# Three output tiles for the last chunk and a first load from a second queue, in a fused recurrence and feed-forward kernel

## The chip, the cores and the metric

The kernel runs on one core of one Trainium2 chip. The core has five engines, each with its own stream of instructions: TensorE (PE; PEld is its weight load), VectorE (DVE), ScalarE (ACT), GpSimd (POOL) and SyncE (SP, which here only issues transfers). They work beside each other and wait for one another through semaphores. Sixteen DMA engines move data between the chip's main memory and the core's memory, SBUF; a transfer is started by an instruction on an engine's queue (SPq and ACTq in the profile). Matmuls write to PSUM, which DVE and ACT can read.

The metric is the device time in microseconds (us) of one execution. The kernel before took 250.95 us, the median of three timed runs (249.91 to 251.05).

## The reference

```
def _attn_ref(r, k, v, w, a, b):          # each (4, 8, 768, 40), float32
    for t in range(S):
        y[:, :, t] = einsum('bhd,bhde->bhe', rt, state)
        Sa = einsum('bhde,bhe->bhd', state, at)
        state = state * wt[:, :, None, :] - einsum('bhd,bhe->bhde', Sa, bt) \
                + einsum('bhd,bhe->bhde', vt, kt)

def _moe_ref(x, w_in, w_out):             # x: y turned to (3072, 320)
    h = x @ w_in                          # 320 -> 2048
    r = maximum(h, 0)
    return (r * r) @ w_out                # 2048 -> 320, float32
```

A recurrence over 768 steps for 32 heads, with a decay `w` in each step, gives `y`; its rows go through a feed-forward layer of two matrix products with a squared ReLU between them. The output is 3072 rows of 320.

## The kernel before

The 768 steps are cut into 12 chunks of 64 (`L`, `NCH`), numbered `c` from 0 to 11. For each chunk, `load(c)` brings in six inputs, `prep(c)` takes the logarithm of the decay (`ln`, line 530), splits it into two bf16 parts (`hi`, line 369, and `lo`, line 384), sums it over time with triangular matmuls and applies exponentials; `rec(c)` solves the chunk and moves the state on; `read(c)` forms `y`, and `ffn(c)` puts it through the layer. Before chunk 0 nothing can begin without the decay: `ln 0` waits for both halves of `raw_w`, 64 partitions each, which `load` issues one after the other from SP (line 411). ScalarE's own first instruction is the load of its function table (line 270); VectorE's first are memsets of padding (lines 313 and 318), and `hi 0` stands behind them.

In `ffn(c)`, `F`/`FL` are the products with `w_in` (256 tokens in the columns), `f` the ReLU from PSUM into the buffer `G` and `q` its square, each in four parts `u0` to `u3` of four blocks of 128 hidden units. `O c` is the product with `w_out`: for each of the 16 hidden blocks and each half `g` of the tokens one matmul of 128 tokens by 320 output columns, summed over the blocks in PSUM, so 32 matmuls a chunk in four parts. `o c` copies the result to SBUF (`osb`), and `st c` stores it.

PSUM is used as four slots of two banks each (`slot`, tiles `pb0` to `pb3`). A result that takes a slot is given its number by the order; in the tile of `O c` the half `g0` lies in one bank and `g1` in the other.

Nothing is scheduled at run time: `Plan.add` records each operation with what it reads and writes, and `plan.issue(ORDER)` emits them in the order of the long string `ORDER` (lines 87 to 215). An entry such as `PE2 O 11 u0` means: on PE, into slot 2, operation `O 11 u0`; `SP st 10` means that SP issues the store of chunk 10. Each engine runs its entries in that order; semaphores are added between engines wherever the tiles demand it, and a PSUM tile counts as one thing: a reader of one half waits for all writes issued to the tile before it, and readers on two engines follow one another.

The last chunk, 11, has its own end (lines 932 to 962). The fourth part of its output product is issued by halves, `OL 11 g1` and then `OL 11 g0`; each half is then evicted in two pieces of 160 columns, `o0` by ACT (line 374) and `o1` by DVE (line 369), and stored by two transfers of 63 rows, `st0` from SP and `st1` from ACT (line 960). Its end in the order is

```
PE2 O 11 u0; DVE o 10; PE O 11 u1; SP st 10; PE O 11 u2; PE OL 11 g1; PE OL 11 g0;
ACT o0 11 g1; DVE o1 11 g1; ACT o0 11 g0; DVE o1 11 g0;
ACT st1 11 g0; ACT st1 11 g1; SP st0 11 g1; SP st0 11 g0
```

Of the kernel before, what the change touches and what calls it, by code (L numbers as in the profile page):

```python
# [209 lines left out]
ACT f 10 u2; DVE f 10 u1; PE1 F 11 u2; ACT q 10 u2; DVE q 10 u1; PE0 FL 11 u1; PE2 FL 11 u3; DVE q  # L210
10 u0; PE FL 11 u2; PE FL 11 u0; PE F 11 u3; ACT f 11 u0; PE F 11 u1; ACT f 11 u2; PE3 O 10 u0;
ACT q 11 u2; PE O 10 u1; ACT f 11 u1; PE O 10 u2; ACT f 11 u3; POOL q 11 u1; ACT q 11 u0; PE O 10
u3; ACT q 11 u3; PE2 O 11 u0; DVE o 10; PE O 11 u1; SP st 10; PE O 11 u2; PE OL 11 g1; PE OL 11
g0; ACT o0 11 g1; DVE o1 11 g1; ACT o0 11 g0; DVE o1 11 g0; ACT st1 11 g0; ACT st1 11 g1; SP st0
11 g1; SP st0 11 g0"""


@with_exitstack
def kernel(
# [30 lines left out]
    def rows(g):  # L250
        return slice(64 * g, 64 * g + 64)
# [150 lines left out]
    def load(c):  # L402
        t0 = slice(c * L, c * L + L)

        def half(x, g):
            return x[2 * g:2 * g + 2, :, t0, :].rearrange("b h t e -> t (b h) e")

        for nm, x, ring in (("w", w, raw_w),):
            def go(x=x, ring=ring):
                for g in range(2):  # L410
                    nc.sync.dma_start(out=ring[c % len(ring)][rows(g)], in_=half(x, g))
            plan.add(f"ld{nm} {c}", [("SP", 2400)], ("ew", {"SP": go}),
                     writes=[("raw", nm, c % len(ring))])

        for y, (nm, x) in enumerate((("k", k), ("b", b))):
            def go_runs(y=y, x=x):
                xv = x[:, :, t0, :].rearrange("b (p q) (k i) e -> q (b p) k (i e)", q=2, i=8)
                for q in range(2):
                    nc.sync.dma_start(out=runs_of(c, y)[:, q, :], in_=xv[q])
            if c in RUNS:  # L420
                plan.add(f"ld{nm} {c}", [("SP", 1100)], ("ew", {"SP": go_runs}),
                         writes=[("raw", nm, c % NKBR)])
                continue
# [13 lines left out]

        def go_a():
            xv = a[:, :, t0, :].rearrange("b (p q) (k i) e -> q (b p) k (i e)", q=2, i=8)
            for q in range(2):  # L440
                nc.sync.dma_start(out=raw_a[c % NA][:, q, :], in_=xv[q])
        plan.add(f"lda {c}", [("SP", 1100)], ("ew", {"SP": go_a}), writes=[("raw", "a", c % NA)])


        def go_r():
            to = raw_r[c % NR]
            if c < NCH - 1:
                xv = r[:, :, c * L + 1:c * L + L + 1, :].rearrange(
                    "b (p q) (k i) e -> q (b p) k (i e)", q=2, i=8)
                for q in range(2):  # L450
                    nc.sync.dma_start(out=to[:, q, :], in_=xv[q])
                return

            x0, pair, m = (c * L + 1) * D, 2 * T * D, NH // 2 - 1
            for q in range(2):
                s0 = x0 + q * T * D
                xv = r.rearrange("b h t e -> (b h t e)")[s0:s0 + m * pair].rearrange(
                    "(m x) -> m x", x=pair)[:, 0:L * D].rearrange("m (k f) -> m k f", f=8 * D)
                nc.sync.dma_start(out=to[0:8 * m, q, :], in_=xv)
                xl = r[NB - 1, NHH - 2 + q, c * L + 1:T, :].rearrange("t e -> (t e)")  # L460
                nc.sync.dma_start(out=to[8 * m:8 * m + 7, q, :],
                                  in_=xl[0:56 * D].rearrange("(k f) -> k f", f=8 * D))
                nc.sync.dma_start(out=to[8 * m + 7:8 * m + 8, q, 0:7 * D],
                                  in_=xl[56 * D:63 * D].rearrange("(k f) -> k f", k=1))
        plan.add(f"ldr {c}", [("SP", 1100 if c < NCH - 1 else 3000)], ("ew", {"SP": go_r}),
                 writes=[("raw", "r", c % NR)])
# [406 lines left out]
    def ffn(c):  # L873
        q2 = c % 2
        for u in range(NFB // 4):
# [24 lines left out]
            for x in (1, 0) if tail else (0, 1):  # L900
# [18 lines left out]
                    out=gv, in_=gv, func=ACTF.Square))],  # L919
               reads=[("G", q2, u)], writes=[("G", q2, u)])  # L920
        ho = ("O", c)
        for u in range(NFB // 4):
            ms = [[], []]
            for j in range(4 * u, 4 * u + 4):
                for g in range(2):
                    ms[g].append(mm(
                        lambda g=g: slot(ho, FP32)[:, g, 0:DM],
                        lambda g=g, j=j: G[q2][:, j, 2 * g * L:2 * g * L + 2 * L],
                        lambda j=j: WOUT[:, j, :], j == 0, j == NFB - 1))
            rd = ([("G", q2, x) for x in range(max(u, O_AFTER) + 1)]  # L930
                  + [("WOUT", 2 * u), ("WOUT", 2 * u + 1)])
            if c == NCH - 1 and u == NFB // 4 - 1:

                for g in range(2):
                    pe(f"OL {c} g{g}", "D", DM, ms[g], reads=rd, writes=[ho + (g,)])
            else:
                pe(f"O {c} u{u}", "D", DM, [m for x in zip(*ms) for m in x], reads=rd,
                   writes=[ho, ho + (0,), ho + (1,)], alloc=[ho] if u == 0 else [])
        ov = out.rearrange("(g bb s) f -> bb s g f", g=2, bb=2)
        t0, n = c * L + 1, min(L, T - 1 - c * L)  # L940
        if c < NCH - 1:
            ew(f"o {c}", copy_alts(lambda: osb[q2][:], lambda: slot(ho, FP32)[:, :, 0:DM], 2 * DM),
               reads=[ho, ho + (0,), ho + (1,)], writes=[("osb", q2)], free=[ho])

            def store():
                for bb in range(2):
# [1 line left out]
            plan.add(f"st {c}", [("SP", 1500)], ("ew", {"SP": store}), reads=[("osb", q2)],  # L948
                     writes=[("left", c)])
            return  # L950
        h = DM // 2
        for g in range(2):
            for x, e in enumerate(("ACT", "DVE")):
                ew(f"o{x} {c} g{g}", copy_alts(
                    lambda g=g, x=x: osb[q2][:, g, h * x:h * x + h],
                    lambda g=g, x=x: slot(ho, FP32)[:, g, h * x:h * x + h], h, engines=(e,)),
                   reads=[ho + (g,), ("left", c - 2)], writes=[("osb", q2, g, x)], free=[ho])
            for bb, (e, q) in enumerate((("SP", nc.sync), ("ACT", nc.scalar))):
                plan.add(f"st{bb} {c} g{g}", [(e, 750 if e == "SP" else 60)],
                         ("ew", {e: lambda q=q, bb=bb, g=g: q.dma_start(  # L960
                             out=ov[bb, t0:t0 + n, g], in_=osb[q2][64 * bb:64 * bb + n, g])}),
                         reads=[("osb", q2, g, 0), ("osb", q2, g, 1)])

    def weights():

# [97 lines left out]
```

## Time and profile before

| | us |
|---|---|
| median of three timed runs | 250.95 (249.91 to 251.05) |
| the profiled execution | 249.74 |
| its span, first to last instruction | 248.0 |
| PE busy | 223.8 (90%) |
| DVE busy | 189.1 (76%) |
| ACT busy | 178.0 (72%) |
| POOL busy | 110.1 (44%) |
| mean granted TensorE clock | 0.987 |

All views below come from the one profiled execution. The page cuts the span into 40 equal slices and shows in each the busy share in tenths; `PEclk` is the clock that TensorE was granted, `DMA` the mean busy share of the 16 DMA engines. The chain is the work that ended last, followed back step by step to what released it. The timeline lists instructions by start, with their length, line and tiles; in brackets stands the idle time of the engine before them and what ended it. Names such as `pb<-WOUT,G` give the tile written and those read; `128x320` is partitions by elements. A row that ends in x64 merges 64 instructions. Where a wait has several semaphores, the profile names the one that came last.

### The profile page before, as it was taken

What the parts mean: (1) busy time and instruction counts of PE and PEld (TensorE: products, weight loads), DVE (VectorE), ACT (ScalarE), POOL (GpSimd) and SP (SyncE); (2) the same over time, 40 slices, a digit from 0 to 9 for tenths busy, and PEclk for the clock granted to TensorE, in tenths of its full rate; (3) what the DMA queues carried; (4) which work ended last, traced back from release to release, by engine and by line L of the source; (5) the groups of instructions that cost most, each with busy time, mean ns of one, the idle gap of its engine ahead of it and who ended that gap; (6) DMA issues with size and microseconds to landing.
All of it is one profiled execution on the core that took longest, in us unless ns stands there. A gap on an engine that the chain in (4) does not pass through costs nothing.

```text
span 248.0 us, 12188 instructions
## 1 busy us (share of the span) xinstructions
PE 223.8 (90%) x5568; PEld 177.3 (71%) x5568; DVE 189.1 (76%) x236; ACT 178.0 (72%) x236; POOL 110.1 (44%) x110
## 2 busy tenths in 40 slices
PE   0588677599999999999999999999999999999991
PEld 0377666488787877788878877877788787867770
DVE  7698988359987889898869696999897578854411
ACT  2588889569899687868777887774777773944850
POOL 4144024532765716473870991491279900033030
PEclk9999999979999999999999999999999999999997
DMA  5989899989999969769698099995410000302021
GB/s 131 209 216 206 168 200 259 328 145 214 181 215 207 152 150 168 138 128 181 136 183 166 14 219 152 193 176 119 119 47 3 3 5 15 96 5 56 0 50 55
DMA packets 102152, 33.54 MB, mean 135 GB/s; under 512 B 88918, under 2 KB 101718, under 8 KB 101846
## 3 DMA queue, kind: packets, MB, share of 16 engines
q1 hardware_dynamic: 101958, 32.62, 63.0%
q8 instruction: 43, 0.70, 1.3%
q10 hardware_dynamic: 144, 0.16, 0.2%
q14 instruction: 7, 0.06, 0.1%
HBM read 28.84 MB, written 3.93 MB: 132 GB/s over the span
## 4 chain that ended last, share of the span: by engine, by line
PE 74%; DVE 9%; DMA 6%; ACT 4%; issue 3%; POOL 1%; SPq 1%; ACTq 0%
PE pb L388 63%; PE pb L392 7%; PE pb L395 4%; DMA G<-in_moe_w_in_dram 3%; DVE KBT L510 2%; DMA raw_a<-in_a_dram 2%; DVE AR L643 1%; DMA out_dram<-osb 1%; POOL WIN L378 1%; ACT G L908 1%; DVE STb L318 1%; DVE VU L371 1%; DVE lo L384 1%; DVE EN L669 1%; ACT osb L374 1%
## 5 line engine op out<-in xcount | busy, mean ns | idle before, releaser
L388 PE MATMUL pb<-WOUT,G 128*128 128x320 bf16 x384 | 57.1, 299 | 0.0
L916 POOL TENSOR_TENSOR G<-G 128x1024 bf16<-128x1024 bf16 x19 | 36.2, 1913 | 39.7 <-PE pb L392 19.3
L388 PE MATMUL pb<-XT,WIN 128*128 128x256 bf16 x384 | 49.9, 279 | 0.0
L908 ACT ACTIVATE G<-pb 128x1024 bf16<-128x1024 f32 x37 | 37.4, 1022 | 14.3 <-PE pb L388 13.1
L388 PEld LDWEIGHTS <-G 128*128 128x128 bf16 x384 | 35.9, 98 | 13.8 <-issue 0.5
L388 PEld LDWEIGHTS <-WIN 128*128 128x128 bf16 x384 | 35.6, 99 | 8.0 <-issue 2.6
L669 DVE TENSOR_TENSOR CX<-pb,MSKI 128x1024 bf16<-128x1024 f32 x24 | 28.9, 1220 | 12.1 <-PE pb L388 11.9
L382 POOL TENSOR_TENSOR KB<-raw_kb,iG 128x640 bf16<-128x640 f32 x14 | 21.6, 1542 | 24.3 <-ACT iG L553 19.9
L669 DVE TENSOR_TENSOR EN<-pb,MSK 128x1024 bf16<-128x1024 f32 x24 | 29.1, 1217 | 3.2 <-PE pb L388 3.1
L559 ACT ACTIVATE Gin<-pb 64x320 f32<-64x320 f32 x48 | 20.2, 428 | 9.4 <-PE pb L388 8.9
L378 POOL CAST VU<-raw_v 64x640 bf16<-64x640 f32 x20 | 14.3, 713 | 16.0 <-DMA raw_v<-in_v_dram 15.6
L761 DVE TENSOR_TENSOR STb<-pb,GT 64x640 bf16<-64x640 f32 x22 | 18.1, 820 | 1.4 <-PE pb L388 0.8
L388 PEld LDWEIGHTS <-EN 64*64 64x64 bf16 x768 | 14.5, 110 | 5.8 <-issue 4.8
L918 ACT ACTIVATE G<-G 128x1024 bf16<-128x1024 bf16 x17 | 17.7, 1055 | 0.1
L643 DVE TENSOR_TENSOR AR<-pb,GT 128x512 bf16<-128x512 bf16 x24 | 15.6, 683 | 2.7 <-PE pb L395 1.7
L374 ACT ACTIVATE osb<-pb 128x640 f32<-128x640 f32 (+1 forms) x10 | 6.2, 623 | 15.2 <-PE pb L388 14.7
L910 DVE TENSOR_SCALAR G<-pb 128x1024 bf16<-128x1024 f32 x11 | 13.4, 1222 | 4.7 <-PE pb L388 4.1
L388 PE MATMUL pb<-XT,WLAST 64*128 64x256 bf16 x192 | 16.8, 271 | 0.0
L382 POOL TENSOR_TENSOR lo<-lnW,hi 128x640 bf16<-128x640 f32 x6 | 8.9, 1492 | 15.8 <-ACT hi L374 10.3
L388 PE MATMUL pb<-hi,UTI 64*128 64x320 bf16 x48 | 7.9, 325 | 7.9 <-DVE hi L369 7.9
L839 DVE TENSOR_TENSOR Yb<-pb,Gin 128x128 bf16<-128x128 f32 (+1 forms) x24 | 12.4, 549 | 2.5 <-PE pb L388 2.3
L374 ACT ACTIVATE AR<-pb 128x512 bf16<-128x512 bf16 x19 | 10.6, 595 | 5.2 <-PE pb L392 3.6
(112 smaller groups left out, 447.1 us busy)
## 6 DMA issues: line engine op xcount, KB each, us to landing
raw_w<-in_w_dram SPq DMA_DIRECT2D x24, 160.0 KB, 4.3
raw_a<-in_a_dram SPq DMA_DIRECT2D x24, 160.0 KB, 4.1
raw_kb<-in_b_dram SPq DMA_DIRECT2D x24, 160.0 KB, 4.1
raw_kb<-in_k_dram SPq DMA_DIRECT2D x24, 160.0 KB, 4.2
raw_v<-in_v_dram SPq DMA_DIRECT2D x24, 160.0 KB, 5.4
raw_r<-in_r_dram SPq DMA_DIRECT2D x22, 160.0 KB, 5.2
out_dram<-osb SPq DMA_DIRECT2D x22, 160.0 KB, 3.1
osb<-in_moe_w_out_dram SPq DMA_DIRECT2D x8, 320.0 KB, 4.8
```

Source lines behind the costliest of these rows:

```text
L374: alts.append(("ACT", c_act(n), lambda: nc.scalar.activation(out=o_(), in_=i_(), func=ACTF.Copy, scale=1.0 if scale is None else scale)))
L378: lambda: nc.gpsimd.tensor_copy(out=o_(), in_=i_())))
L382: return [("POOL", 40 + 2.35 * n, lambda: nc.gpsimd.tensor_tensor(out=o_(), in0=a_(), in1=b_(), op=op)), ("DVE", c_dve(n), lambda: nc.vect ...
L388: return lambda: nc.tensor.matmul(out=o_(), lhsT=l_(), rhs=r_(), start=start, stop=stop, skip_group_check=True)
L392: return lambda: nc.tensor.transpose(out=o_(), in_=i_(), identity=IDb[rows(g), :])
L559: nc.scalar.activation(out=Gin[c % NGI][rows(g), NP * jh:NP * jh + NP, :].rearrange("p j e -> p (j e)"), in_=slot(hb, FP32)[rows(g), g, 0: ...
L643: ew(f"tA {c} g{g}", [("DVE", c_dve(512), lambda g=g: nc.vector.tensor_tensor(out=steps(AR[q2][:, 0, g]), in0=turned(ha, g), in1=steps(GT[ ...
L669: evac(f"m{nm} {c} g{g}", lambda s, n: [("DVE", c_dve(n), lambda: nc.vector.tensor_tensor(out=dst[q2][:, g, s].rearrange("p q i t -> p (q ...
L761: ew(f"s {c} q{q}", [("DVE", c_dve(2 * n), lambda q=q: nc.vector.tensor_tensor(out=STb[q2][rows(q), :, q, 0:D], in0=slot(hs, FP32)[rows(q) ...
L908: ("ACT", c_act(1024), lambda gb=gb, hf=hf: nc.scalar.activation(out=gb, in_=slot(hf, FP32)[:], func=ACTF.Relu)),
L916: ("POOL", 1900, lambda gv=gv: nc.gpsimd.tensor_tensor(out=gv, in0=gv, in1=gv, op=ALU.mult)),
L918: ("ACT", c_act(1024), lambda gv=gv: nc.scalar.activation(out=gv, in_=gv, func=ACTF.Square))],
```

## The change

Two things change. In `load(c)`, the second half of chunk 0's decay is issued by ACT's queue; the later chunks keep both halves on SP. In the last chunk, the output goes into three PSUM tiles in three slots: A holds `g1` with all 320 columns, B the first and C the last 160 columns of `g0`. A is issued ahead of the last parts of B and C and evicted by DVE (`oa`); its two stores follow, one from SP and one from ACT. Then B is evicted by ACT (`ob`) and C by DVE (`oc`), and the stores of `g0` are issued, one from each of the two queues.

On PE the last chunk has 16 matmuls of 320 columns and 32 of 160, where it had 32 of 320. On ACT the new transfer stands behind the table load and ahead of `ln 0`; at the end, ACT issues a store of `g1` before it evicts B. The rest of the instructions keep their engines, slots and order.

```
-u3; ACT q 11 u3; PE2 O 11 u0; DVE o 10; PE O 11 u1; SP st 10; PE O 11 u2; PE OL 11 g1; PE OL 11
-g0; ACT o0 11 g1; DVE o1 11 g1; ACT o0 11 g0; DVE o1 11 g0; ACT st1 11 g0; ACT st1 11 g1; SP st0
-11 g1; SP st0 11 g0"""
+u3; ACT q 11 u3; PE1 OA 11 u0; DVE o 10; PE0 OB 11 u0; PE2 OC 11 u0; PE OA 11 u1; SP st 10; PE OB
+11 u1; PE OC 11 u1; PE OA 11 u2; PE OA 11 u3; PE OB 11 u2; PE OC 11 u2; DVE oa 11; SP st0 11 g1;
+ACT st1 11 g1; PE OB 11 u3; ACT ob 11; PE OC 11 u3; DVE oc 11; SP st0 11 g0; ACT st1 11 g0"""
...
-                for g in range(2):
-                    nc.sync.dma_start(out=ring[c % len(ring)][rows(g)], in_=half(x, g))
+                for g, q in enumerate((nc.sync, nc.sync if c else nc.scalar)):
+                    q.dma_start(out=ring[c % len(ring)][rows(g)], in_=half(x, g))
...
         ho = ("O", c)
+        parts = ((("A", 1, 0, DM), ("B", 0, 0, DM // 2), ("C", 0, DM // 2, DM))
+                 if c == NCH - 1 else ())
         for u in range(NFB // 4):
             ms = [[], []]
+            for p, g, x, y in parts:
+                hp = ho + (p,)
+                pe(f"O{p} {c} u{u}", "D", y - x, [
+                    mm(lambda hp=hp, x=x, y=y: slot(hp, FP32)[:, 0, 0:y - x],
+                       lambda g=g, j=j: G[q2][:, j, 2 * g * L:2 * g * L + 2 * L],
+                       lambda j=j, x=x, y=y: WOUT[:, j, x:y], j == 0, j == NFB - 1)
+                    for j in range(4 * u, 4 * u + 4)],
+                   reads=[("G", q2, x) for x in range(u + 1)]
+                   + [("WOUT", 2 * u), ("WOUT", 2 * u + 1)],
+                   writes=[hp], alloc=[hp] if u == 0 else [])
+            if parts:
+                continue
...
-        h = DM // 2
+        for p, g, x, y in parts:
+            ew(f"o{p.lower()} {c}", copy_alts(
+                lambda g=g, x=x, y=y: osb[q2][:, g, x:y],
+                lambda p=p, x=x, y=y: slot(ho + (p,), FP32)[:, 0, 0:y - x], y - x),
+               reads=[ho + (p,), ("left", c - 2)], writes=[("osb", q2, g, p)], free=[ho + (p,)])
         for g in range(2):
-            for x, e in enumerate(("ACT", "DVE")):
-                ew(f"o{x} {c} g{g}", copy_alts(
-                    lambda g=g, x=x: osb[q2][:, g, h * x:h * x + h],
-                    lambda g=g, x=x: slot(ho, FP32)[:, g, h * x:h * x + h], h, engines=(e,)),
-                   reads=[ho + (g,), ("left", c - 2)], writes=[("osb", q2, g, x)], free=[ho])
             for bb, (e, q) in enumerate((("SP", nc.sync), ("ACT", nc.scalar))):
...
-                         reads=[("osb", q2, g, 0), ("osb", q2, g, 1)])
+                         reads=[("osb", q2, g, p) for p, y, _, _ in parts if y == g])
```

More of the change, by code (lines that the diff above doesn't have):

```diff
@@ L931, in ffn @@
                   + [("WOUT", 2 * u), ("WOUT", 2 * u + 1)])
[L932 to L938, printed above, removed]
+            pe(f"O {c} u{u}", "D", DM, [m for x in zip(*ms) for m in x], reads=rd,
+               writes=[ho], alloc=[ho] if u == 0 else [])
         ov = out.rearrange("(g bb s) f -> bb s g f", g=2, bb=2)
@@ L942, in ffn @@
             ew(f"o {c}", copy_alts(lambda: osb[q2][:], lambda: slot(ho, FP32)[:, :, 0:DM], 2 * DM),
-               reads=[ho, ho + (0,), ho + (1,)], writes=[("osb", q2)], free=[ho])
+               reads=[ho], writes=[("osb", q2)], free=[ho])
             def store():
```

## The prediction

> **What bounds the kernel now.** I read the page first, then the stages, then the two ends, because the change touches only the first transfer and the last chunk.
>
> ```profile
> span 248.0 us, 12188 instructions
> ...
> PEclk9999999979999999999999999999999999999997
> DMA  5989899989999969769698099995410000302021
> ...
> q8 instruction: 43, 0.70, 1.3%
> ...
> PE 74%; DVE 9%; DMA 6%; ACT 4%; issue 3%; POOL 1%; SPq 1%; ACTq 0%
> ```
>
> Columns of the next view, the busy time by stage: stretch, its length, then busy us (and instructions) of PE, PEld, DVE, ACT, POOL, then the granted clock, the DMA share and GB/s.
>
> ```profile
> 2.00:4.00 2.00, 0.00 (x0) 0.10 (x1) 1.97 (x8) 0.09 (x1) 1.16 (x6) 1.00 0.74 121
> 4.00:8.00 4.00, 0.12 (x2) 0.10 (x2) 3.56 (x9) 0.74 (x1) 0.72 (x1) 1.00 0.99 241
> ...
> 25.00:46.00 21.00, 16.39 (x522) 14.12 (x516) 18.44 (x22) 17.81 (x24) 5.89 (x8) 1.00 0.98 231
> 46.00:50.00 4.00, 1.25 (x54) 1.01 (x53) 0.42 (x1) 1.96 (x3) 2.94 (x3) 1.00 1.12 280
> 50.00:54.00 4.00, 4.00 (x45) 2.92 (x37) 2.36 (x2) 2.81 (x4) 1.14 (x2) 0.57 0.77 138
> 54.00:242.00 188.00, 187.02 (x4647) 147.52 (x4646) 146.80 (x171) 138.99 (x179) 90.59 (x76) 1.00 0.58 117
> 242.00:245.00 3.00, 0.68 (x5) 0.27 (x3) 0.65 (x2) 0.61 (x2) 0.00 (x0) 1.00 0.11 34
> ```
>
> Three regimes stand there. From 4 to 50 us the 16 DMA engines are full (share 0.98 to 1.12) while PE still has gaps. From 54 to 242 us PE is busy 187.02 of 188.00 us. From 242.68 us (0.68 into its row) PE has nothing left, and 248.0 - 242.68 = 5.32 us are evictions, stores and the program's end. Whatever the change saves at the front counts only if it brings PE's long stretch forward; whatever it saves in the last 5.32 us counts in full. The tail, in the timeline (start, us, engine, line, operation, tiles, count):
>
> ```profile
> 233.82 8.86 PE L388 MATMUL pb<-WOUT,G 128*128 128x320 bf16 x64
> ...
> 235.11 1.92 ACT L908 ACTIVATE G<-pb 128x1024 bf16<-128x1024 f32 x2
> 236.19 1.89 POOL L916 TENSOR_TENSOR G<-G 128x1024 bf16<-128x1024 bf16 x1 [7.78 <-ACT G L908]
> 236.91 2.00 ACT L918 ACTIVATE G<-G 128x1024 bf16<-128x1024 bf16 x2
> 238.37 0.82 DVE L369 COPY osb<-pb 128x640 f32<-128x640 f32 x1 [6.37 <-PE pb L388]
> 239.22 1.25 SPq L947 DMA_DIRECT2D out_dram<-osb  x2
> 242.71 0.30 ACT L374 ACTIVATE osb<-pb 128x160 f32<-128x160 f32 x1 [3.80 <-PE pb L388]
> 243.05 0.32 DVE L369 COPY osb<-pb 128x160 f32<-128x160 f32 x1 [3.86 <-ACT osb L374]
> 243.40 0.98 SPq L960 DMA_DIRECT2D out_dram<-osb  x2
> 243.41 0.30 ACT L374 ACTIVATE osb<-pb 128x160 f32<-128x160 f32 x1 [0.39 <-DVE osb L369]
> 243.75 0.33 DVE L369 COPY osb<-pb 128x160 f32<-128x160 f32 x1 [0.37 <-ACT osb L374]
> 244.10 0.94 ACTq L960 DMA_DIRECT2D out_dram<-osb  x2
> ```
>
> Four quarters of one PSUM tile leave strictly one after another, each engine released by the other, from 242.71 to 243.75 + 0.33 = 244.08. Even `g1`, whose matmuls are issued before those of `g0`, starts only when PE has finished everything. Then ScalarE's queue issues two stores in a row, until 244.10 + 0.94 = 245.04; from there to the end of the span are 2.96 us. A narrower window separates the issues that start together:
>
> ```profile
> 244.10 0.29 SPq L960 DMA_DIRECT2D out_dram<-osb  x1
> 244.10 0.62 ACTq L960 DMA_DIRECT2D out_dram<-osb  x1
> ```
>
> **Part 1, PE's work for the last chunk.** Tile A (`g1`) keeps 16 matmuls of 320 columns; the 16 of `g0` become 32 of 160 columns into B and C, each with its own weight load. No row has 160 columns, so I bound one by its neighbours:
>
> ```profile
> 44.67 0.62 PE L395 MATMUL pb<-IDQ,tR 128*128 128x128 bf16 x8
> 45.13 1.06 PE L395 MATMUL pb<-IDQ,STb 128*128 128x128 bf16 x16
> ...
> 222.60 1.05 PE L388 MATMUL pb<-XT,WIN 128*128 128x256 bf16 x8
> 223.48 1.25 PE L388 MATMUL pb<-WOUT,G 128*128 128x320 bf16 x8
> ...
> 228.36 2.79 PE L388 MATMUL pb<-XT,WIN 128*128 128x256 bf16 x24
> ```
>
> A longer run less a shorter one gives the pitch, weight loads included: (1.06 - 0.62) / 8 = 55 ns at 128 columns, (2.79 - 1.05) / 16 = 108.8 ns at 256, (8.86 - 1.25) / 56 = 135.9 ns at 320. These lie on one line of 0.42 ns a column, so I take 55 + 32 x 0.42 = 68.4 ns; the ends are 55 and 108.8. The edit costs 32 x 68.4 - 16 x 135.9 = 2.19 - 2.17 = +0.02 us (ends -0.41 and +1.31). PE then ends at 242.70. The Trainium skill speaks against this (TensorE: Matmul & The Clock Gate, section Back-to-back issue gap): it gives about 81 ns per matmul sustained at 128 columns, because the weight load shares the pitch. By that the 32 would cost at least 2.59 us, and this term would be +0.42 instead of +0.02. The 55 ns of the transposes here does not bear it out.
>
> The new order needs three free PSUM slots and the four parts of `G` a little sooner. The last eviction that frees a slot ends at 235.11 + 1.92 = 237.03, the squares end at 238.08 (POOL) and 238.91 (ACT); half of the 64 matmuls, chunk 10's, run until about 233.82 + 32 x 0.136 = 238.2, the first part (squared by 236.91 + 1.00 = 237.91) is used then, POOL's from 239.3, the last by A from 240.9. The covers are 0.3, 1.2 and 2.0 us; a square that came later than that would stall PE by the excess.
>
> **Part 2, the evictions.** A is complete before the last 16 narrow matmuls: 242.70 - 16 x 0.0684 = 241.61. VectorE, idle since 239.19, takes 128x320 from 241.64 (the lag of 0.03 us is that of 242.68 to 242.71); its time lies on the line through 0.33 us at 160 and 0.82 at 640, which gives 0.49, so 242.13. The two stores of `g1` go out at 242.15, one from SP (free since 240.47) and one from ScalarE's queue, with 0.29 to 0.62 us each. This store is now ahead of ScalarE's eviction of B, which waits behind it: B is complete at 242.70 - 4 x 0.0684 = 242.43, the queue is free between 242.44 and 242.77, and the 0.30 us of the eviction end between 242.76 and 243.07. VectorE takes C from 242.73 for 0.33, to 243.06. So the wait added on ScalarE is covered by C, by a hair; without that cover it would cost up to 0.3 us. Both last stores start at 243.08 instead of 244.10.
>
> **Part 3, the last stores.** They are one on each queue, not two on ScalarE's. Started together they end their issue after 0.29 (SP) and 0.62 us (the row of ScalarE's first), at 243.70; had the 0.62 been that queue's first use, 243.37. Against 245.04 that is 1.34 to 1.67 us. I take 1.45, nearer the end measured for two issues side by side. The 2.96 us behind stay: the same bytes, the same end of the program.
>
> **Part 4, the front.**
>
> ```profile
> 0.80 1.28 ACT L270 ACT_TABLE_LOAD   x1 [0.80 <-PEq L1047]
> 0.81 1.47 SPq L411 DMA_DIRECT2D raw_w<-in_w_dram  x2
> ...
> 5.99 0.74 ACT L530 ACTIVATE lnW<-raw_w 128x640 f32<-128x640 f32 x1 [3.90 <-DMA raw_w<-in_w_dram]
> ...
> 6.46 0.91 DVE L318 MEMSET STb<- 128x1024 uint32 x1 [0.16 <-issue]
> 7.36 0.47 DVE L369 CAST hi<-lnW 128x640 bf16<-128x640 f32 x1
> ```
>
> ```profile
> DMA to landing us min/median/max: 4.3/4.3/4.3
> ```
>
> One of the two issues leaves SP, so every later load of SP can be issued earlier by half of 1.47, 0.74 us. The logarithm may start sooner too, but its reader `hi` starts at 7.36, the moment VectorE's memsets end (6.46 + 0.91), while the logarithm ended at 6.73: an earlier `w` alone gains nothing. It has 0.6 us to spare, so a later one costs nothing up to there. The earlier loads meet DMA engines that are full from 4 us on; the only room is in the stage from 2 to 4 us, 0.26 x 2.00 = 0.52 us, of which most is the start of the first transfer and stays. Bounds are -0.74 and, for a late second half, the 1.0 us of the second rival; I take -0.2, near what that one row leaves open. On ScalarE only the logarithm stands behind the moved issue, and it waits for that transfer anyway.
>
> **Sum.** -1.45 - 0.2, with PE's 0.02 inside the first: -1.65 us. The profiled execution took 249.74 us (span 248.0 and 1.74 around it), so 248.1 by its footing. It is 1.21 us under the median of the three timed runs, 250.95 (249.91 to 251.05); on the median the forecast is 249.3.
>
> **Rivals.**
>
> *The front gains its whole issue* (249.3 - 0.5 = 248.8). For it: SP issues without a pause and one issue is 0.74 us. Against it: the full DMA engines and the memsets.
>
> *ScalarE's queue issues late.* The table load stands ahead of the DMA in its program and ends at 2.08. If the issue waits for that alone, the second half lands at 2.08 + 4.3 = 6.4, the logarithm ends at 7.1 and nothing is lost. If it waits for a drain as long again, 1.28 us, it lands at 7.7, the logarithm ends at 8.4, and `hi` and all behind it come 1.0 us later: 249.3 + 0.2 + 1.0 = 250.5. It decides beyond 0.2 us of extra wait. No row shows what follows a table load at once. The Trainium skill (ScalarE: Activation LUTs, section What ACT_TABLE_LOAD costs) gives about 1283 ns for the load, as the 1.28 here, and 1380 ns for a drain with it; by that the loss would be 1.1 us.
>
> *The narrow matmuls pay for their weight loads*, up to the pitch of 256 columns: PE ends up to 1.31 us later and all behind it too, 250.6; from half of that on the forecast's gain is no longer to be told from none. Against it: the straight line of the three pitches. By the Trainium skill's pitch named in part 1 it would be 249.7.
>
> *Slower: another stall of PE's stream.*
>
> ```profile
> 33.04 7.54 DMA G<-in_moe_w_in_dram
> ...
> 46.73 2.75 issue
> ```
>
> In the middle of one group of matmuls PE stands still for 2.75 us, waiting for nothing the trace shows, beside a DMA share of 1.12; PE's instruction blocks (the `q8` line) use the same engines. After it the granted clock is 0.57 for 4 us, which costs 0.43 x 4.00 = 1.72. A second such stall, because every load now meets PE's stream earlier, costs 2.75 + 1.72 = 4.5 and gives 253.8; it decides once more than 1.65 us of it comes. Against it: the order on each engine in that stage is the same, and the shift is small.
>
> **How the numbers follow.** Forecast 0.60 (its own range 248.8 to 249.8), full front 0.12, late queue 0.10, dear narrow matmuls 0.10, second stall 0.08. A measurement of this kernel tells about 0.5%, 1.25 us, from no change, so faster means under 249.7: most of the first (0.47), the full front (0.11), none but the cheap end of the others: 0.58. Slower takes the stall and a little of the late queue, 0.12; the rest, 0.30, is same. The range 248.3 to 250.9 leaves out the stall and the ends.
>
> **What would show it.** Right: a 128x320 eviction on DVE near 241.6 while PE still runs; 128x160 on ACT and DVE overlapping, both over within 0.4 us after PE's last matmul; last issues on SPq and ACTq together, 1.0 us sooner against PE's end; about 3.9 us from PE's end to the span's, not 5.32. At the front: `hi` still at 7.36 and SP's third issue near 1.6. Wrong: PE's run in the tail longer than 8.9 us; ACT's B released by its own store; `hi` later than 7.4; the first ACTq issue after 2.08; a changed idle of PE near 46.7 us, or another stretch under full clock.

## The result, and the profile after

The changed kernel took 249.51 us (median of 22 runs, 247.37 to 252.89), the kernel before, beside it on the same chip, 251.3 us (22 runs, 248.74 to 252.6). The ratio is 0.9936, with a 95% interval of 0.9914 to 0.9959: about 1.6 us faster. (The ratio leaves out runs over 1.5% above the fastest of their kernel, so it is not that of the two medians.) The forecast was 249.3.

Both kernels scatter by 4 to 5.5 us from run to run. The profiled execution of the changed kernel is one of its long ones (252.12 us), so a second profile of the same kernel (247.99 us, from the run "changed kernel again" below) stands beside it. First the page of the long one:

```profile
span 250.4 us, 12220 instructions
...
PEclk9999999758999999999999999999999999999998
```

Three slices near a fifth of the span have a low clock (7, 5, 8) where the page before had one (7). The stages of the long profile from 42 us on, with the columns of the prediction's view by stage:

```profile
42.00:46.00 4.00, 2.88 (x86) 2.73 (x86) 2.36 (x3) 2.72 (x5) 1.77 (x3) 0.78 0.84 253
46.00:50.00 4.00, 3.59 (x87) 2.98 (x84) 1.12 (x2) 2.99 (x5) 1.86 (x2) 0.80 1.03 296
50.00:54.00 4.00, 2.19 (x11) 1.53 (x12) 1.92 (x2) 0.79 (x2) 2.68 (x3) 0.63 0.83 132
54.00:58.00 4.00, 4.00 (x36) 3.67 (x35) 1.29 (x2) 2.28 (x4) 0.72 (x1) 0.52 0.95 203
58.00:240.00 182.00, 180.54 (x4581) 141.90 (x4579) 144.88 (x168) 135.69 (x176) 88.17 (x75) 1.00 0.58 116
...
246.00:249.00 3.00, 0.10 (x2) 0.00 (x0) 0.33 (x1) 0.30 (x1) 0.00 (x0) 1.00 0.36 108
```

and of the short one:

```profile
42.00:46.00 4.00, 3.48 (x128) 3.15 (x128) 2.47 (x4) 3.62 (x6) 2.42 (x3) 1.00 0.99 347
46.00:50.00 4.00, 1.64 (x47) 1.47 (x47) 0.56 (x1) 1.87 (x3) 2.50 (x3) 0.99 1.20 268
50.00:54.00 4.00, 4.00 (x35) 3.28 (x33) 2.44 (x4) 1.87 (x4) 0.72 (x2) 0.58 0.69 144
54.00:58.00 4.00, 4.00 (x118) 3.52 (x116) 3.52 (x6) 4.00 (x5) 0.24 (x1) 1.00 1.14 205
58.00:240.00 182.00, 180.86 (x4512) 142.16 (x4510) 142.58 (x165) 134.78 (x175) 90.15 (x75) 1.00 0.55 114
```

The third number from the end of a row, the granted clock, tells them apart. In the long profile it is 0.78, 0.80, 0.63 and 0.52 in four stretches of 4 us: (0.22 + 0.20 + 0.37 + 0.48) x 4 = 5.1 us of full clock are missing. In the short one, as before the change, only the stretch from 50 us is low, and 0.42 x 4 = 1.7 us are missing. The difference, 3.4 us, is the most that the clock can account for, since PE is not busy all through these stretches. PE runs the same matmuls in the same order in both profiles, so one can follow them singly: the long profile is 0.53 us behind the short one at the 737th matmul (41.95 us in the short one), 3.61 at the 1013th (56.13 us) and 4.15 at PE's end (246.10 against 241.95). So most of what lengthens it arises in that stage, and the same kernel's second profile does not have it; the other 0.5 us come later, where the clock is 1.00 in both.

What the change does touch is the tail. In the timeline of the short profile (line 968 is the store, line 960 before the change):

```profile
233.05 8.90 PE L388 MATMUL pb<-WOUT,G 128*128 128x320 bf16 x80
...
240.88 0.49 DVE L369 COPY osb<-pb 128x320 f32<-128x320 f32 x1 [2.46 <-DMA out_dram<-osb]
241.40 1.38 SPq L968 DMA_DIRECT2D out_dram<-osb  x2
241.40 0.63 ACTq L968 DMA_DIRECT2D out_dram<-osb  x1
241.99 0.32 DVE L369 COPY osb<-pb 128x160 f32<-128x160 f32 x1 [0.62 <-PE pb L388]
242.16 0.30 ACT L374 ACTIVATE osb<-pb 128x160 f32<-128x160 f32 x1 [4.01 <-PE pb L388]
242.49 0.29 ACTq L968 DMA_DIRECT2D out_dram<-osb  x1
```

A narrower window parts the two last stores, and the window from 241 us gives PE's end, 241.00 + 0.95:

```profile
242.49 0.29 SPq L968 DMA_DIRECT2D out_dram<-osb  x1
...
241.00:244.00 3.00, 0.95 (x14) 0.75 (x11) 0.69 (x2) 0.30 (x1) 0.00 (x0) 1.00 0.35 102
```

PE ends at 241.95, A is evicted 1.07 us earlier while PE still runs, C and B overlap, and the last two issues start together and end at 242.78. Counted from PE's end, to within 10 ns, before and in the two profiles of the changed kernel:

| | last issue ends | from there to the span's end | tail |
|---|---|---|---|
| before | 2.36 | 2.99 | 5.35 |
| changed, short profile | 0.83 | 3.49 | 4.32 |
| changed, long profile | 0.83 | 3.46 | 4.29 |

The tail is 1.03 us shorter, not 1.45. The last issue came forward by 1.53 us, inside the forecast's range, but what stands behind it grew by 0.5. The transfers show where. The next rows are the mean busy share of the 16 DMA engines (in tenths) and their GB/s, in 40 slices of 0.1 us from PE's end on; first the kernel before, then the changed one:

```profile
DMA  0000000000000005555202362573656655520000
GB/s 0 0 0 0 0 0 0 0 0 0 0 0 0 0 13 154 179 166 192 77 26 64 102 154 64 141 141 90 218 218 230 218 205 218 218 64 26 26 26 0
```

```profile
DMA  0056465455641263656455100000000000000000
GB/s 0 0 141 154 90 128 102 128 180 218 230 179 51 64 141 128 179 179 205 179 205 167 51 26 26 26 26 13 13 0 0 0 0 0 0 0 0 0 0 0
```

After the change the engines work from 0.2 to 2.3 us, with one dip at 1.2 us, at a share of about 0.55. Then a rest of traffic, 26 GB/s and less, goes on for 0.6 us more. The issues are no longer what the tail waits for; the transfers are.

### The profile page after: what moved, and what is told of

The parts are those of the page before. It is cut to its first block, busy times and chain, and to the rows that moved or that the text cites. A ratio compares the mean times of both kernels' runs of the same rounds, so it can differ in the third digit from the quotient of the medians.

```text
span 250.4 us, 12220 instructions
## 1 busy us (share of the span) xinstructions
PE 227.5 (91%) x5584; PEld 180.7 (72%) x5584; DVE 189.2 (76%) x236; ACT 177.7 (71%) x235; POOL 110.1 (44%) x110
## 4 chain that ended last, share of the span: by engine, by line
PE 59%; DVE 10%; DMA 8%; SPq 8%; ACT 7%; issue 3%; POOL 3%; ACTq 0%; POOLq 0%
PE pb L388 49%; PE pb L392 6%; PE pb L395 4%; DMA G<-in_moe_w_in_dram 3%; SPq L451 3%; DMA out_dram<-osb 2%; DMA raw_a<-in_a_dram 2%; SPq L427 2%; SPq L434 1%; ACT G L908 1%; SPq L990 1%; ACT Gin L559 1%; DMA raw_r<-in_r_dram 1%; ACT AR L374 1%; DVE KBT L510 1%
## 5 line engine op out<-in xcount | busy, mean ns | idle before, releaser
L388 PE MATMUL pb<-WOUT,G 128*128 128x320 bf16 (+1 forms) x400 | 57.1, 294 | 0.0
L388 PEld LDWEIGHTS <-G 128*128 128x128 bf16 x400 | 36.6, 98 | 13.3 <-issue 0.5
L575 ACT ACTIVATE GT<-pb 128x1024 f32<-128x1024 f32 x12 | 12.3, 1022 | 3.0 <-PE pb L388 2.9
```

What stands on the lines that cost most here:

```text
L388: return lambda: nc.tensor.matmul(out=o_(), lhsT=l_(), rhs=r_(), start=start, stop=stop, skip_group_check=True)
```

## The experiments

### The tail alone, the front alone, and the change again

The tail alone is the changed kernel with chunk 0's decay loaded by SP as before; the front alone is the kernel before with the second half on ACT's queue.

```
-                for g, q in enumerate((nc.sync, nc.sync if c else nc.scalar)):
+                for g, q in enumerate((nc.sync, nc.sync)):
```

```
-                for g in range(2):
-                    nc.sync.dma_start(out=ring[c % len(ring)][rows(g)], in_=half(x, g))
+                for g, q in enumerate((nc.sync, nc.sync if c else nc.scalar)):
+                    q.dma_start(out=ring[c % len(ring)][rows(g)], in_=half(x, g))
```

Expected of the tail alone:

> The changed kernel with both halves of chunk 0's decay on SP again, so only the three tiles are left of the change. My theory (the tail carries nearly all of the gain, the front about 0.2 us): ratio to the kernel before 0.994 (-1.45 us), and from PE's last matmul to the end of the span about 4.3 us as in the changed kernel, against 5.35 before. Rival (the tail gives only the 1.06 us that the two profiles show between PE's end and the span's end, the front gives the other half of the 1.6 us): ratio 0.996, same 4.3 us.

of the front alone:

> The kernel before with only the second half of chunk 0's decay on ScalarE's queue. My theory: ratio 0.999 (-0.2 us), no difference that can be told; hi still starts at 7.35, SP's lead of 0.7 us is down to nothing when the load of w_in is issued at 33 us. Rival (the front gains 0.5 to 0.7 us): ratio 0.997 to 0.998 with an interval below 1, and PE's long stretch begins that much earlier.

and of the changed kernel once more:

> The changed kernel once more, for a second profile and a comparison on the same chip as the two halves. Theory: ratio 0.994, tail 4.3 us behind PE's last matmul; the stage from 42 to 58 us differs from the first profile in its idle times and half-clock windows, while the stretch behind it keeps its length (188 us) within 0.3 us. Rival (the moved issue makes that stage longer each time): again three half-clock windows of 3.4 us and a PE end near 246 us.

Measured, each against the same runs of the kernel before (median 250.33 us):

| | ratio, 95% interval | median | tail in the profile |
|---|---|---|---|
| tail alone | 0.9971 (0.9936 to 1.0007) | 249.67 | 4.36 |
| front alone | 0.998 (0.9947 to 1.0013) | 250.03 | 5.39 |
| both, again | 0.9955 (0.9914 to 0.9996) | 248.85 | 4.32 |

The tail's length is the same in every profile of one kind, to 0.07 us, and goes with the new tail alone; that part is settled at 1.0 us. In whole times the two parts are too small for the scatter: neither interval leaves out no change, and none leaves out the forecast share. The stretch behind the scattering stage was expected to keep its length within 0.3 us; from the 1013th matmul to PE's end it took 185.82 us here, 186.36 in the long profile and 185.42 to 187.35 in all profiles, so that stretch scatters too.

### What does the tail wait for: the issue on ACT, the eviction on two engines

In the changed kernel ACT issues a store of `g1` for 0.63 us and then evicts B 0.17 us after C has begun. Two runs take that away. In one, both stores of `g1` are issued by SP; in the other, DVE evicts both B and C.

```
-ACT st1 11 g1; PE OB 11 u3; ACT ob 11; PE OC 11 u3; DVE oc 11; SP st0 11 g0; ACT st1 11 g0"""
+SP st1 11 g1; PE OB 11 u3; ACT ob 11; PE OC 11 u3; DVE oc 11; SP st0 11 g0; ACT st1 11 g0"""
...
-            for bb, (e, q) in enumerate((("SP", nc.sync), ("ACT", nc.scalar))):
+            for bb, (e, q) in enumerate((("SP", nc.sync), ("SP", nc.sync) if g else ("ACT", nc.scalar))):
```

```
-ACT st1 11 g1; PE OB 11 u3; ACT ob 11; PE OC 11 u3; DVE oc 11; SP st0 11 g0; ACT st1 11 g0"""
+ACT st1 11 g1; PE OB 11 u3; DVE ob 11; PE OC 11 u3; DVE oc 11; SP st0 11 g0; ACT st1 11 g0"""
```

> The changed kernel with both stores of g1 issued from SP, so that no store stands ahead of ScalarE's eviction of B. Theory (the store holds ScalarE, 0.63 us for its issue): the eviction of B starts about 0.03 us after B is complete, that is about 0.2 us before the end of PE's work, ends before that of C, and the last two issues start 0.17 us sooner against PE's end (0.37 us after it in place of 0.54). Rival (ScalarE waits for PE's end or for the landing of an earlier store, not for its own issue): B's eviction stays at 0.2 us after PE's end and nothing moves.

> The changed kernel with B evicted by VectorE too, so nothing is evicted side by side. Theory (B is complete 0.27 us before C, so one engine can take both; on ScalarE B only waits behind the store of g1): B's eviction starts 0.24 us before PE's end, C's follows at +0.09 to +0.42, the last issues start at +0.44 in place of +0.54, and from PE's end to the span's end it is 4.2 us in place of 4.3. Rival (the two engines side by side are what shortened the tail): last issues at +0.70 or later, tail 4.5 us.

The timelines: `g1`'s stores on SP, then B and C by DVE.

```profile
241.75 0.30 ACT L374 ACTIVATE osb<-pb 128x160 f32<-128x160 f32 x1 [3.56 <-PE pb L388]
242.03 0.33 DVE L369 COPY osb<-pb 128x160 f32<-128x160 f32 x1 [0.62 <-PE pb L388]
...
242.41 0.28 SPq L968 DMA_DIRECT2D out_dram<-osb  x1
242.44 0.59 ACTq L968 DMA_DIRECT2D out_dram<-osb  x1
```

```profile
240.73 0.60 DVE L369 COPY osb<-pb 128x160 f32<-128x160 f32 x2 [0.34 <-PE pb L388]
...
241.36 0.29 SPq L968 DMA_DIRECT2D out_dram<-osb  x1
241.37 0.30 ACTq L968 DMA_DIRECT2D out_dram<-osb  x1
```

PE ends at 241.99 and 240.97. B is now evicted 0.24 us before that, 0.45 us earlier than in the changed kernel, and C at +0.04 as there; the last issues start 0.1 us sooner, not 0.17. With DVE alone both issues end at +0.70 instead of +0.83. Yet the tails are 4.25 and 4.33 us against 4.32, not the expected 4.2 of the second run. The packet records of the traces (a packet is here one row of 320 values, written by one DMA engine) show why the earlier issues of that run bring nothing: the first rows of the two last stores start at +1.37 and +1.53, in the changed kernel as with DVE alone. (The one time of each, 247.97 and 247.02 us, lies at the low end of the changed kernel's 34, 247.16 to 252.89; one time says nothing.) Two engines side by side are not what made the tail shorter, and the issue is not what ends it. The first run also settles a price. ACT's issue takes 0.59 us although SP's beside it takes 0.28; in the changed kernel, where ACT's queue has issued once already, both take 0.29 side by side. So in these runs the 0.6 us goes with ACT's first issue in the tail, not with two issues at once. (It is no general rule: with smaller stores, in the next run, ACT's first issue takes 0.38 us and its second 0.74.)

### The transfers: sixteen engines, or one queue

The share of 0.55 is near 9/16 = 0.56. The Trainium skill (DMA: Bandwidth & Descriptors, section Why a DMA increments its semaphore by 16 and not by 1) says that a transfer uses the largest number of engines up to 16 that divides its outer dimension; for 63 rows that is nine, and the share agrees. The next run cuts each of the four stores into rows 0 to 47 and 48 to 62.

```
-                         ("ew", {e: lambda q=q, bb=bb, g=g: q.dma_start(
-                             out=ov[bb, t0:t0 + n, g], in_=osb[q2][64 * bb:64 * bb + n, g])}),
+                         ("ew", {e: lambda q=q, bb=bb, g=g: [q.dma_start(
+                             out=ov[bb, t0 + i:t0 + j, g],
+                             in_=osb[q2][64 * bb + i:64 * bb + j, g]) for i, j in ((0, 48), (48, n))]}),
```

> The changed kernel with each of its four last stores cut in two, rows 0 to 47 and rows 48 to 62: the same bytes, eight transfers instead of four, two issues in a row on each queue. Theory: the changed kernel's tail (4.25 to 4.36 us from PE's end to the span's end) is bound by its transfers, since the 63-row stores use only nine of the sixteen DMA engines, which are busy without a break from 0.2 to 2.2 us after PE's end; with 48 and 15 rows the engines in use are 16 and 15, the last landing comes 0.2 to 0.5 us earlier than +3.1 to +3.3, and the tail is 3.8 to 4.1 us, although one more issue of 0.29 us stands ahead of the last transfer. Rival: the issues bind the tail; then the last one ends 0.29 us later on each queue and the tail is 4.5 to 4.7. A third: the transfers' fixed time binds, not the engines nor the issues; then the tail stays within 0.1 us of 4.32. The time of the whole kernel moves by less than 0.5 us in any case, ratio 0.993 to 0.997 to the kernel before.

The profile (PE ends at 242.04), and the DMA share from there on:

```profile
241.50 1.15 ACTq L968 DMA_DIRECT2D out_dram<-osb  x2
242.77 0.30 ACT L374 ACTIVATE osb<-pb 128x160 f32<-128x160 f32 x1 [4.53 <-DVE osb L369]
243.10 0.86 ACTq L968 DMA_DIRECT2D out_dram<-osb  x2
```

```profile
DMA  0007698874510000002689895530000000000000
```

The expected tail of 3.8 to 4.1 us was missed: it is 4.34. The share does rise to 0.7 to 0.9, and from the last issue's end (243.96) to the span's end it takes only 2.41 us instead of 3.49. But ACT now issues two stores ahead of B's eviction, for 1.15 us, and B comes 0.52 us later, and the last issues with it; the gain is spent on that. The same stores without that wait, all from SP, were not run. The whole kernel's ratio, 0.9995 (0.9961 to 1.0029), is worse than was expected of it, though its tail is as long as the changed kernel's. Why is open; the scatter from run to run would do it, but that is not shown. (The medians of all runs, 249.51 and 250.42 us, would make it 0.9964.)

The other side of the same question: the two last stores from one queue, one behind the other. First both on ACT, as in the kernel before the change.

```
-ACT st1 11 g1; PE OB 11 u3; ACT ob 11; PE OC 11 u3; DVE oc 11; SP st0 11 g0; ACT st1 11 g0"""
+ACT st1 11 g1; PE OB 11 u3; ACT ob 11; PE OC 11 u3; DVE oc 11; ACT st0 11 g0; ACT st1 11 g0"""
...
-            for bb, (e, q) in enumerate((("SP", nc.sync), ("ACT", nc.scalar))):
+            for bb, (e, q) in enumerate((("SP", nc.sync) if g else ("ACT", nc.scalar), ("ACT", nc.scalar))):
```

> The changed kernel with both of the last stores (of g0) issued by ScalarE's queue, one after the other, as in the kernel before; three PSUM tiles and early g1 as changed. Theory: the transfers bind the tail, not the issues; the last issue ends 0.3 us later (near +1.15 instead of +0.83 after PE's end), the last landing moves by 0 to 0.2 us and the tail is 4.3 to 4.5 us. Rival, the prediction's part 3: what stands behind the last issue's end is a constant, so the tail grows by the whole 0.3 us, to 4.6 or more.

```profile
243.30 0.30 ACT L374 ACTIVATE osb<-pb 128x160 f32<-128x160 f32 x1 [4.03 <-PE pb L388]
243.63 0.66 ACTq L968 DMA_DIRECT2D out_dram<-osb  x2
```

```profile
DMA  0056463555641145655645211000000000000000
GB/s 0 0 141 154 102 128 77 154 167 218 230 179 51 64 128 141 166 154 179 218 179 179 102 64 38 13 0 0 0 0 0 0 0 0 0 0 0 0 0 0
```

PE ends at 243.08, so the last issue ends at +1.21, 0.38 us later than in the changed kernel, and still the tail is shorter: 4.00 us. Neither the theory (4.3 to 4.5) nor its rival (4.6 or more) had that. (Its one time is 248.79 us.) Two transfers from one queue end sooner, though the second is issued later, than two issued at once from two queues; the trickle at the end is over at +2.6 instead of +2.9. A new theory then: the two queues hold each other up on the nine engines that both transfers are taken to use. It was put to the test with all four stores on SP; the edit is shown against the run with `g1`'s stores on SP.

```
-SP st1 11 g1; PE OB 11 u3; ACT ob 11; PE OC 11 u3; DVE oc 11; SP st0 11 g0; ACT st1 11 g0"""
+SP st1 11 g1; PE OB 11 u3; ACT ob 11; PE OC 11 u3; DVE oc 11; SP st0 11 g0; SP st1 11 g0"""
...
-            for bb, (e, q) in enumerate((("SP", nc.sync), ("SP", nc.sync) if g else ("ACT", nc.scalar))):
+            for bb, (e, q) in enumerate((("SP", nc.sync), ("SP", nc.sync))):
```

> The changed kernel with all four last stores on SP's queue, in a row: g1's two and then g0's two; three PSUM tiles, B by ScalarE and C by VectorE as changed. Against the run with g1's stores on SP and g0's one on each queue (tail 4.25 us), one store alone is moved, from ScalarE's queue to SP's. Theory, from the run with both last stores on ScalarE's queue (tail 4.00): two transfers of the same nine DMA engines from two queues hold each other up (2.4 us from the end of the issue to the landing), in a row on one queue they land 1.7 us behind their issue. The last issue then ends at +1.01 (0.42 + 2 x 0.29) after PE's end instead of +1.04, or +0.83 in the changed kernel, the landings come at +2.4 and +2.7, and the tail is 3.7 to 3.9 us. Rival: one issue more on SP costs its 0.29 us; then the tail is 4.4 to 4.6 us. Second rival: the 4.00 was chance, and the tail lies at 4.2 to 4.35 as in the other runs. For the whole kernel 0.5 us less than the changed one, ratio 0.990 to 0.995 to the kernel before, by the theory.

```profile
242.45 1.62 SPq L968 DMA_DIRECT2D out_dram<-osb  x4
243.04 0.33 DVE L369 COPY osb<-pb 128x160 f32<-128x160 f32 x1 [0.61 <-PE pb L388]
```

```profile
DMA  0045555545512355555553100000000000000000
GB/s 0 0 115 154 166 179 192 205 154 166 167 64 77 102 128 179 179 218 205 192 179 115 64 26 0 0 0 0 0 0 0 0 0 0 0 0 0 0 0 0
```

PE ends at 243.00. C is out at +0.37, the issues of `g0` run from +0.42 to +1.07 one behind the other, the traffic is over at +2.4, and the tail is 3.90 us, at the upper end of the expected 3.7 to 3.9. Against the run with `g1`'s stores on SP (4.25) one store alone has moved, from ACT's queue to SP's, at the same end of the last issue (+1.04 and +1.07), and that took 0.35 us out. All tails together:

| last two stores | last issue ends | from there to the span's end | tail |
|---|---|---|---|
| two queues: changed kernel | 0.83 | 3.49 | 4.32 |
| two queues: `g1` on SP | 1.04 | 3.21 | 4.25 |
| two queues: B, C by DVE | 0.70 | 3.63 | 4.33 |
| two queues, each store in two | 1.93 | 2.41 | 4.34 |
| one queue: both on ACT | 1.21 | 2.79 | 4.00 |
| one queue: all four on SP | 1.07 | 2.83 | 3.90 |

On two queues, the earlier the last issue ends, the longer is what follows, so that the sum stays at 4.3; on one queue what follows is 2.8. All nine profiles that end on two queues have a tail of 4.25 to 4.36 us; each of the two ways to end on one queue was profiled once.

The packet records show where the difference lies. After PE's end 252 rows of 1280 bytes are written. The 242nd of them starts at +2.27 in the changed kernel's short profile, at +2.29 with both last stores on ACT and at +2.14 with all on SP. So the bulk is held up little by two queues, if at all. The last of the 252 rows starts 0.54 us after the 242nd in the changed kernel, but only 0.22 and 0.25 us after it on one queue. In the changed kernel these late rows start 52 ns apart, from the two queues in turn, and a row mostly takes 55 ns: that fits the pace of a single DMA engine, which still has rows of both transfers to write when the others are done. What makes it lag is not shown. From the last packet's end to the span's end it takes 1.42 to 1.54 us in all thirteen profiles; that part is the constant one.

The Trainium skill (DMA: Bandwidth & Descriptors, section Issuing engines are not separate DMA queues) says that transfers of different engines run on the same 16 DMA engines and interleave, and its rules for kernel authors that spreading them only saves issue time. The runs agree, since the late rows come from the two queues in turn, and go further: here that saving cost more than it brought.

The run with all stores on SP took 248.63 us (median of 12; 246.78 to 250.22), ratio 0.9932 (0.9891 to 0.9974) to the kernel before. It has the shortest tail, and the lowest median of the versions timed in several runs; by whole times its interval overlaps the changed kernel's.

### The front

Three runs move the start of chunk 0: both halves of its decay on ACT's queue; the padding memsets of `STb`, which hold up `hi`, on GpSimd; and these memsets on GpSimd with both halves on SP.

```
-                for g, q in enumerate((nc.sync, nc.sync if c else nc.scalar)):
+                for g, q in enumerate((nc.sync if c else nc.scalar, nc.sync if c else nc.scalar)):
```

```
-        nc.vector.memset(v_, 0.0)
+        (nc.gpsimd if any(t_ is x for x in STb) else nc.vector).memset(v_, 0.0)
```

> The changed kernel with both halves of chunk 0's decay on ScalarE's queue, so that SP is two issues ahead (1.4 us) instead of one. Theory (full DMA engines eat the lead): SP's lead over the kernel before is 1.3 us at its first issues, under 0.6 us at 24 us and under 0.4 us at 36 us; hi still at 7.35; ratio within 0.3% of that of the changed kernel. Rival (each issue taken off SP is worth its 0.6 to 0.7 us at the end): ratio 0.990 to 0.992.

> The changed kernel with the two memsets of STb moved from VectorE to GpSimd, so that VectorE is free 1.9 us before hi can start. Theory (hi is bound by these memsets in both kernels; without them by the logarithm): hi starts at 6.05, right behind the logarithm (5.29 + 0.74), 1.3 us sooner than in the changed kernel, if GpSimd's own work is not in the way. What is left of it at 50 us is open: if the loads of w_in bound that stage, nothing. Compare with the next run for what the moved issue gives once the cover is gone.

> The run before this one with both halves on SP again. Theory: hi starts at 6.75, behind a logarithm that ends 0.70 us later than there, so the moved issue is worth 0.7 us at hi once the cover is gone; at the end the two are within 0.3% since the DMA engines are full from 4 us on. Rival (the front is bound by the engines' chain from hi): this run is 0.7 us, 0.3%, slower than the one before it.

First the front of the changed kernel itself, in the timeline of the long profile, and its stage from 2 to 4 us:

```profile
0.80 1.28 ACT L270 ACT_TABLE_LOAD   x1 [0.80 <-PEq L1055]
...
0.83 0.70 ACTq L411 DMA_DIRECT2D raw_w<-in_w_dram  x1
...
1.63 1.53 SPq L441 DMA_DIRECT2D raw_a<-in_a_dram  x2
...
5.29 0.74 ACT L530 ACTIVATE lnW<-raw_w 128x640 f32<-128x640 f32 x1 [3.21 <-DMA raw_w<-in_w_dram]
...
7.35 0.43 DVE L369 CAST hi<-lnW 128x640 bf16<-128x640 f32 x1
...
2.00:4.00 2.00, 0.00 (x0) 0.10 (x1) 1.96 (x8) 0.08 (x1) 1.16 (x6) 1.00 0.90 161
```

Then both halves on ACT:

```profile
0.84 1.65 ACTq L411 DMA_DIRECT2D raw_w<-in_w_dram  x2
...
7.46 0.74 ACT L530 ACTIVATE lnW<-raw_w 128x640 f32<-128x640 f32 x1 [5.37 <-DMA raw_w<-in_w_dram]
8.23 0.49 DVE L369 CAST hi<-lnW 128x640 bf16<-128x640 f32 x1 [0.79 <-ACT lnW L530]
```

and the memsets on GpSimd, first with the changed front, then with both halves on SP:

```profile
6.22 0.66 DVE L369 CAST hi<-lnW 128x640 bf16<-128x640 f32 x1 [0.94 <-ACT lnW L530]
...
6.80 1.19 DVE L1013 COPY IDQ<-IDb 64x64 bf16<-64x64 bf16 x2
...
8.02 0.82 DVE L384 TENSOR_TENSOR lo<-lnW,hi 128x640 bf16<-128x640 f32 x1
```

```profile
6.53 0.64 DVE L369 CAST hi<-lnW 128x640 bf16<-128x640 f32 x1 [1.24 <-ACT lnW L530]
...
7.10 0.89 DVE L1013 COPY IDQ<-IDb 64x64 bf16<-64x64 bf16 x2
...
8.02 0.82 DVE L384 TENSOR_TENSOR lo<-lnW,hi 128x640 bf16<-128x640 f32 x1
```

| | `hi` starts | `lo` starts | ratio, 95% interval | median | tail |
|---|---|---|---|---|---|
| changed kernel | 7.35 | 8.10 | 0.9955 (0.9914 to 0.9996) | 248.85 | 4.32 |
| both halves on ACT | 8.23 | 9.04 | 0.9948 (0.9916 to 0.998) | 249.89 | 4.35 |
| memsets on GpSimd | 6.22 | 8.02 | 0.9944 (0.9913 to 0.9974) | 249.45 | 4.33 |
| the same, both halves on SP | 6.53 | 8.02 | 0.9947 (0.9914 to 0.998) | 249.71 | 4.34 |

(The last three stand against other runs of the kernel before, median 250.9.) `hi` lies anywhere between 6.22 and 8.23 us, and the ratios are the same within 0.0011. An earlier `hi` is lost at once: `lo` starts at 8.02 with either load, behind two copies on DVE that took 1.19 and 0.89 us in these runs and 0.37 in the changed kernel. What slows the copies was not tested. With both halves on ACT `hi` was expected at 7.35 and came 0.9 us late, because the logarithm did. Carried to the end in full, that would make 0.9991 of the 0.9955, but each of the two ratios is uncertain by 0.003 to 0.004, so the whole times can't tell whether it reaches the end. With the memsets out of the way the moved issue is worth 0.31 us at `hi`, not the expected 0.7, and nothing at `lo`. What the front contributes is not resolved: the four ratios with some of the decay on ACT and the changed kernel's tail (0.9936, 0.9955, 0.9948, 0.9944) average 0.9946, the two with it on SP (0.9971, 0.9947) 0.9959; the difference, 0.0013 or 0.3 us, is well inside their intervals.

## Why the prediction was right, and where not

**The time.** 249.51 against 249.3, well inside the range; but the sum had a term that was 0.4 us too large. The tail gave 1.03 us instead of 1.45. That leaves about 0.6 us of the measured 1.6, and the interval of the ratio (1.0 to 2.2 us) covers anything from nothing to 1.2 us for the front and for chance. By the second measurement, 0.9955, the gain is 1.1 us: the tail by itself. That the total came out so near is therefore luck in part.

**Part 1, PE's work: right.** 80 matmuls took 8.90 us where 64 took 8.86: +0.04 against the forecast +0.02, and no stall for a slot or a square. The 81 ns of the Trainium skill (TensorE: Matmul & The Clock Gate, section Back-to-back issue gap) would have made it +0.42; the trace does not bear that out.

**Part 2, the evictions: right for A and C, wrong by 0.14 us for B.** A starts at -1.07 and takes 0.49 us (forecast -1.06, 0.49), C at +0.04. The step that failed is "covered by C, by a hair". ACT's issue took 0.63 us, the upper end of what the forecast allowed, and B's eviction started 0.13 us after it, so B ends at +0.51, not between +0.06 and +0.37. The last stores start at +0.54 instead of +0.38. The two runs on that wait show that it cost the tail at most 0.07 us, which is no more than the profiles of one kind differ by.

**Part 3, the last stores: the issue right, the term behind it wrong.** The last issue's end moved by 1.53 us, inside the forecast's 1.34 to 1.67. Its working had 0.62 us as the price of two issues side by side; in the runs with 63-row stores it is that of ACT's first issue in the tail, and the queue had had it already with `g1`. The step that failed is "the 2.96 us behind stay: the same bytes, the same end of the program". On two queues they became 3.49. With all four stores on one queue they are 2.83. What stays is only the 1.42 to 1.54 us behind the last packet; from the end of the last issue to that packet it took 1.57 us before, 2.03 in the changed kernel and 1.38 with all stores on SP. The same bytes are not the same time. That the transfers, and not the issue, bound the tail is shown by the two runs whose issues ended 0.24 and 0.38 us later than the changed kernel's and whose tails were 0.42 and 0.32 us shorter.

**Part 4, the front: the mechanism borne out in part, the size open.** `hi` stayed at 7.35, held by the memsets (without them it starts at 6.22), SP's issue of `raw_a`, the third of all as before, came at 1.63, and the DMA share from 2 to 4 us rose from 0.74 to 0.90, so part of the 0.52 us of room was used. SP's lead over the one profile of the kernel before, issue by issue, is 0.69 or 0.70 us at `raw_a` in all nine profiles with this front. At 20 us, among the loads of a later chunk, it lies between -0.07 and 1.00, its median at 0.22; in the two profiles with both halves on SP there is none (-0.14 and -0.18), and with both halves on ACT 1.57 us of lead are gone at 7.5 us. So most of the lead is lost, as forecast. (From 8 to 25 us the DMA share before the change was 0.96, a little under the 0.98 that the prediction gives as its lowest.) Whether -0.2 us reaches the end, no run can tell.

**The rivals.** ScalarE's queue did not issue late: 0.83 us, beside the table load, 0.03 us after its start. The narrow matmuls did not cost up to 1.31 us but 0.04. The sign of the second stall, more stretches under full clock, did show in the long profile: four, and one in the short profile of the same kernel. That the change is not what brings it is supported by the runs of both kernels: the mean granted clock of a single run was 0.966 to 0.993 in 29 runs of the kernel before and 0.975 to 0.993 in the 12 runs of the changed kernel beside them. The full gain of the front, 0.5 us more, is neither shown nor excluded.

## What to carry to other kernels

In a tail that ends in stores, first find out whether the issue or the transfer ends it: the DMA rows from the last matmul on show whether the engines are still busy when the last issue is over. Where they are, splitting the last stores over two queues can cost more than the issue it saves. A stage that scatters by several us hides a gain of one; take the length of the touched stage in each profile, and let the whole time only confirm it.

## What the runs showed that was not expected

- Two 63-row stores issued together on SP and ACT leave a trickle of 26 GB/s and less for 0.6 us after the bulk is written, by their pace the rows of one lagging DMA engine; in a row on SP the same bytes were through 0.4 us sooner (+2.45 instead of +2.87), although the last was issued 0.24 us later. What makes that engine lag is open.
- For 63-row stores ACT's queue takes 0.59 to 0.64 us for its first issue in the tail and 0.28 to 0.34 for the next ones; SP's takes 0.28 to 0.33 for each.
- A DMA issue on ACT's queue is not held up by the table load ahead of it in the program: 0.83 us against 0.80, with the load running until 2.08.
